# Sketched attention rebuilt around small TensorE tiles and VectorE transposes, with a 256-token first FFN group

## The chip, the cores and the metric

One core of one Trainium2 chip. The metric is the device time of one execution in microseconds (us). Times are medians over the executions of a kernel, each compared with executions of the kernel before on the same chip in the same rounds. Each run lists the span and clock of one core only, so there is no second die to compare it with, and a run counts as slow only when it lies over 1.5% above the fastest of its own kernel. The kernel before takes 137.7 us.

PE is the TensorE matmul stream, PEld its weight loads, DVE is VectorE, ACT is ScalarE, POOL is GpSimd, and SP is the engine that issues most transfers.

## The reference, cut to what matters

```python
# q, k, v: (4 batches, 4 heads, 1088 tokens, 32); S1, S2: (8, 32), float32
def phi(x):                                   # 8 x 8 = 64 features per token and head
    a = einsum('rd,bhsd->bhsr', S1, x)
    b = einsum('rd,bhsd->bhsr', S2, x)
    return einsum('bhsi,bhsj->bhsij', a, b).reshape(..., 64)
kv  = einsum('bhsf,bhsd->bhfd', phi(k), v)
z   = phi(k).sum(axis=2)
num = einsum('bhsf,bhfd->bhsd', phi(q), kv)
den = einsum('bhsf,bhf->bhs', phi(q), z) + 1e-6
x   = (num / den)                             # -> 4352 tokens x 128
h   = x @ w_in                                # 128 x 2048
out = (h - tanh(h)) @ w_out                   # 2048 x 128
```

All of `k` of a batch must be reduced into `kv` before any numerator of the batch exists, and `num/den` must exist before the feed-forward part (FFN) of those tokens can begin. With a group of 512 tokens, the FFN is 16 matmuls in, 16 tanh on ScalarE, 16 matmuls out, and two for the linear part `x @ w_in @ w_out`.

## The kernel before

The program is written as a list of operations with dependencies. A list scheduler in the kernel file, with a cost for each operation, fixes the order on each engine when the program is built. The list of an engine is its program, with semaphore waits between the operations. So an operation whose data is late holds up what stands behind it in the list.

The parts that the change touches, shortened:

```python
GCOLS = [512] * 8 + [256]          # token groups of the FFN
QG = [(0, 3), (3, 6), (6, 9)]      # pieces of 128-token blocks of one batch
...
bank_h = 3 PSUM banks; bank_o = 1; bank_kv = 1; bank_a = 3      # (names shortened)
...
# k: two sketches one after the other, all 128 rows, 32 columns
for x in range(2):
    pa = _Val(bank_a)
    for g in range(4):
        e.matmul(pa[g*32:(g+1)*32, 0:288], sab[:, x, :], t_[:, c0:c0+288])
    e.transpose(ab[:, x, :], pa[:, 0:288])                 # VectorE
...
# q: three sketches of the whole batch (a, b, and the one for the denominator)
# then for each piece of three blocks:
qp = ap * b                                                # VectorE outer product, 768 columns
for hp in range(2):
    for bi in range(nb):                                   # TensorE transposes with an identity
        e.transpose(tp[:, bi*128:bi*128+kk], qp[0:kk, ...], ident[0:kk, 0:kk])
    copy(qt[:, 0:ncol], tp[:, 0:ncol])                     # ScalarE or VectorE
for hp in range(2):                                        # numerator
    e.matmul(nm[hp*64:(hp+1)*64, 0:ncol], kvb[:, hp, :], qts[hp][:, 0:ncol])
copy(xT[:, col0:col0+ncol], nm[:, 0:ncol])
```

## Time and profile before

| what | measured | view |
|---|---|---|
| time | 137.7 us (137.01 to 138.67 over 5 runs) | times |
| span of the profiled run | 135.4 us | page, first line |
| first tanh | 31.26 us | timeline of ScalarE, chain |
| last output transpose | 131.38 us | timeline of VectorE |
| last numerator burst of batches 2 and 3 | 83.29 and 108.99 us, so 25.7 us a batch | timeline of TensorE |
| TensorE instructions, with weight loads | 982 + 996 = 1978 | page, section 1 |

The page of the kernel before divides the span into 40 slices of 3.4 us. Each digit is the busy share of a slice in tenths, and PEclk is the granted TensorE clock in tenths of full speed:

```profile
PE   0477977598989999999999999999999999989970
PEclk9999986869999999999999999999999999999999
DMA  4999999970406050005000220140003004013043
```

From slice 10 on, until the last two, TensorE is busy for 80% of a slice or more. Before that it often is not, and in slices 6 to 9 its clock is down to 0.8 and 0.6. The table of stretches of the kernel before gives the same with numbers (stretch, its length, then the busy time and count of PE, PEld, DVE, ACT and POOL, the granted clock, the DMA share and GB/s):

```profile
20.00:24.00 4.00, 2.75 (x24) 1.20 (x20) 2.38 (x11) 0.27 (x1) 0.00 (x0) 0.70 1.07 260
48.00:56.00 8.00, 7.95 (x43) 3.81 (x43) 6.04 (x16) 6.44 (x14) 0.00 (x0) 1.00 0.22 34
```

The chain of waits of the kernel before, in order of time, at the end of its start-up (start, duration, what):

```profile
27.48 2.32 PE psa L551 x8
29.80 1.44 PE psa L421 x16
31.26 0.61 ACT th L610
```

So the kernel before is a start-up of 31 us and a TensorE-bound stream of 100 us. The prediction rested on one more reading, the cost of changing between tile shapes on TensorE. This is a burst of 24 matmuls on 32-column tiles in the timeline of PE of the kernel before, amid FFN matmuls that start 0.22 us apart. The burst and its changes of shape take 63.78 − 63.08 = 0.70 us here. The profile puts 0.16 us of it down to a wait for ScalarE, and the prediction seems to leave that part out:

```profile
63.08 0.54 PE L443 MATMUL pskv<-w,v 128*32 128x64 f32 x24
63.78 0.38 PE L619 MATMUL pso<-th,wo 128*128 128x512 bf16 x1 [0.16 <-ACT th L610]
```

### The profile page before, as it was taken

To read this page: it belongs to the slowest core of one execution; us is meant where nothing else is said; L and a number is where in the kernel's file an instruction comes from. 1 tells how busy PE (TensorE), PEld (TensorE's weight loads), DVE (VectorE), ACT (ScalarE), POOL (GpSimd) and SP (SyncE) were. 2 spreads that over 40 slices of the span, in tenths; PEclk is the share of its full clock that TensorE was granted. 3 is DMA by queue.
4 is the path that set the end of the run, shared out by engine and by line. 5 is a ranking of instruction groups with operands and counts; after the bars stand their busy time and mean duration, and the time that the engine had idled before them with its cause. 6 is when DMAs were issued, how large, how long until landed. Compare 5 with 4: busy or idle time off the path is not lost.

```text
span 135.4 us, 2508 instructions
## 1 busy us (share of the span) xinstructions
PE 118.0 (87%) x982; PEld 54.8 (40%) x996; DVE 64.9 (48%) x152; ACT 89.4 (66%) x180; POOL 2.4 (2%) x22
## 2 busy tenths in 40 slices
PE   0477977598989999999999999999999999989970
PEld 0325623533344344434543535345334533333440
DVE  0447256958983698239056904561496131020210
ACT  3031670256964677976558797775579968999960
POOL 7000000000000000000000000000000000000000
PEclk9999986869999999999999999999999999999999
DMA  4999999970406050005000220140003004013043
GB/s 133 264 289 339 293 224 267 222 221 25 168 1 169 0 80 0 0 0 78 5 5 0 44 33 0 19 64 0 0 9 58 15 0 67 11 20 60 0 70 51
DMA packets 25563, 11.18 MB, mean 83 GB/s; under 512 B 18896, under 2 KB 22992, under 8 KB 25552
## 3 DMA queue, kind: packets, MB, share of 16 engines
q1 hardware_dynamic: 25472, 11.02, 34.9%
q8 instruction: 8, 0.13, 0.4%
q14 instruction: 3, 0.02, 0.1%
q10 hardware_dynamic: 80, 0.01, 0.0%
HBM read 8.79 MB, written 2.23 MB: 81 GB/s over the span
## 4 chain that ended last, share of the span: by engine, by line
PE 75%; ACT 11%; DVE 6%; DMA 2%; issue 2%; ACTq 0%
PE pso L619 19%; PE psh L607 19%; ACT th L610 11%; PE psa L551 7%; PE psa L541 7%; PE psa L500 5%; PE psa L421 5%; PE pskv L443 4%; PE pskv L453 3%; PE pso L623 3%; DMA s_86<-in_S_dram 2%; PE pskv L468 1%; PE psa L579 1%; DVE ot L628 1%; PE pskv L470 1%
## 5 line engine op out<-in xcount | busy, mean ns | idle before, releaser
L610 ACT ACTIVATE th<-psh 128x512 bf16<-128x512 f32 (+1 forms) x144 | 71.7, 592 | 19.0 <-PE psh L607 17.3
L607 PE MATMUL psh<-xT,wi 128*128 128x512 bf16 (+1 forms) x137 | 49.0, 368 | 1.2 <-ACT th L610 0.8
L619 PE MATMUL pso<-th,wo 128*128 128x512 bf16 (+1 forms) x138 | 45.5, 368 | 0.8 <-ACT th L610 0.7
L607 PEld LDWEIGHTS psh<-xT,wi 128*128 128x128 bf16 x144 | 13.9, 97 | 19.4 <-ACT th L610 9.6
L619 PEld LDWEIGHTS pso<-th,wo 128*128 128x128 bf16 x144 | 13.5, 99 | 19.1 <-issue 4.8
L628 DVE STREAM_TRANSPOSE ot<-pso 128x512 f32<-128x512 f32 (+1 forms) x9 | 6.1, 683 | 21.9 <-PE pso L619 21.9
L541 PE MATMUL psa<-ident,qp 128*128 128x128 f32 (+1 forms) x72 | 11.7, 289 | 2.5 <-DVE qp L530 2.3
L541 PEld LDWEIGHTS psa<-ident,qp 128*128 128x128 f32 (+1 forms) x72 | 9.0, 147 | 5.9 <-DVE qp L530 2.7
L530 DVE TENSOR_TENSOR qp<-ap,abq 128x768 f32<-128x768 f32 x12 | 11.1, 940 | 0.0
L432 DVE TENSOR_TENSOR w<-abk 128x768 f32<-128x768 f32 x12 | 10.8, 952 | 0.1
L277 DVE COPY qpT<-psa 128x320 f32<-128x320 f32 (+1 forms) x10 | 5.2, 518 | 11.8 <-PE psa L541 11.6
L551 PE MATMUL psa<-qpT,kvb 128*64 128x384 f32 (+1 forms) x48 | 10.0, 526 | 0.0
L504 DVE STREAM_TRANSPOSE abq<-psa 128x288 f32<-128x288 f32 x12 | 5.8, 483 | 7.5 <-PE psa L500 7.5
L443 PE MATMUL pskv<-w,v 128*32 128x64 f32 (+1 forms) x288 | 8.0, 247 | 1.3 <-DVE w L432 1.3
L277 ACT COPY qpT<-psa 128x384 f32<-128x384 f32 (+1 forms) x14 | 6.4, 481 | 3.9 <-PE psa L541 3.8
L443 PEld LDWEIGHTS pskv<-w,v 128*32 128x32 f32 (+1 forms) x288 | 5.4, 122 | 5.6 <-issue 2.9
L277 ACT CAST xT<-psa 128x384 bf16<-128x384 f32 (+1 forms) x10 | 4.6, 463 | 3.7 <-PE psa L551 3.3
L421 PE MATMUL psa<-kTa,sab 128*32 128x288 f32 x32 | 6.0, 483 | 1.1 <-DVE kTb L407 1.1
L570 ACT CAST wi<-wi_f 128x512 bf16<-128x512 f32 x4 | 2.5, 619 | 5.9 <-DMA wi_f<-in_moe_w_in_dram 5.7
L459 DVE TENSOR_TENSOR gm<-pskv,mask_84 32x32 f32<-32x32 f32 x4 | 0.7, 179 | 11.3 <-PE pskv L453 11.3
L421 PE MATMUL psa<-kTb,sab 128*32 128x288 f32 x32 | 6.0, 483 | 0.0
L425 DVE STREAM_TRANSPOSE abk<-psa 128x288 f32<-128x288 f32 x8 | 3.8, 480 | 4.0 <-PE psa L421 4.0
(63 smaller groups left out, 82.2 us busy)
## 6 DMA issues: line engine op xcount, KB each, us to landing
qL<-in_q_dram SPq DMA_DIRECT2D x8, 272.0 KB, 7.1
out_dram<-ot SPq DMA_DIRECT2D x20, 64.0 KB, 2.0
kLa<-in_k_dram SPq DMA_DIRECT2D x4, 288.0 KB, 6.0
v<-in_v_dram SPq DMA_DIRECT2D x8, 144.0 KB, 5.5
kLb<-in_k_dram SPq DMA_DIRECT2D x4, 256.0 KB, 5.3
v<-in_v_dram SPq DMA_DIRECT2D x8, 128.0 KB, 5.7
wi_f<-in_moe_w_in_dram SPq DMA_DIRECT2D x4, 256.0 KB, 5.4
wo_f<-in_moe_w_out_dram SPq DMA_DIRECT2D x4, 256.0 KB, 8.1
```

What stands on the lines that cost most here:

```text
L277: return e.copy(o, i) if name == "scalar" else e.tensor_copy(o, i)
L421: i = e.matmul(pa.ap[g * 32:(g + 1) * 32, 0:288], sab.ap[:, x, :], t_.ap[:, c0:c0 + 288], start=True, stop=True)
L432: P.add("vector", lambda e, n, p=p, wv=wv: e.tensor_tensor(out=wv.ap.rearrange("p (x i j) -> p x i j", i=8, j=8), in0=ab.ap[:, 0, p * 96:( ...
L443: i = e.matmul(kv.ap[h * 32:(h + 1) * 32, 0:64], vt.ap[0:kk, h, blk * 32:(blk + 1) * 32], wv.ap[0:kk, (bi * 4 + h) * 64:(bi * 4 + h + 1) * ...
L500: i = e.matmul(pa.ap[g * 32:(g + 1) * 32, 0:288], s_, qv[:, :, g, :], start=True, stop=True)
L530: P.add("vector", lambda e, n, sl=sl, aq=aq, qp=qp, nx=nx: e.tensor_tensor(out=qp.ap[:, 0:nx * 64].rearrange("p (x i j) -> p x i j", i=8, ...
L541: P.add("tensor", lambda e, n, bi=bi, kk=kk, tp=tp, hp=hp, qp=qp: e.transpose(tp.ap[:, bi * 128:bi * 128 + kk], qp.ap[0:kk, bi * 256 + hp ...
L551: i = e.matmul(nm.ap[hp * 64:(hp + 1) * 64, 0:ncol], kvb.ap[:, hp, :], qts[hp].ap[:, 0:ncol], start=True, stop=True)
L607: P.add("tensor", lambda e, n, jb=jb, hv=hv: e.matmul(hv.ap[:, 0:n_], wi[jb // 4].ap[:, (jb % 4) * 128:(jb % 4 + 1) * 128], xt, start=True ...
L610: P.add("scalar", lambda e, n, hv=hv, th=th: e.activation(out=th.ap[:, 0:n_], in_=hv.ap[:, 0:n_], func=AF.Tanh, scale=-1.0), r=[hv], w=[th ...
L619: fn = lambda e, n, x=x, st=st, sp_=sp_: e.matmul(ov.ap[:, 0:n_], wo[x // 4].ap[:, x % 4, :], ths[x].ap[:, 0:n_], start=st, stop=sp_)
L628: P.add("vector", lambda e, n: e.transpose(ot.ap[:, 0:n_], ov.ap[:, 0:n_]), r=[ov], w=[ot], key=t0, cost=_dve(n_))
```

## The change

The intent is to take attention work off TensorE and to let the FFN begin earlier.

- Both sketches of k (and of q) come from one burst on eight 64x32 tiles that run side by side.
- The denominator comes from a Gram matrix of the two k sketches, gathered over four column groups.
- The outer products of q are transposed in 32x32 blocks by VectorE instead of by TensorE. The numerator is a burst of 64 short matmuls on all sixteen 32x32 tiles.
- Sketches, kv, Gram and numerator share one fixed set of four PSUM banks, `bk[0..3]`. The numerator writes all four.
- The first FFN group has 256 tokens, and q of batch 0 is loaded, sketched and finished in three pieces.
- All loads are queued at the start, since k, v and q have a buffer for every batch. Zero matmuls fill long waits of TensorE.

The diff, cut to its core (the scheduler's new cost tables, `weights()`, the loads and most of the VectorE operations are left out):

```diff
-GCOLS = [512] * 8 + [256]
-QG = [(0, 3), (3, 6), (6, 9)]
+GCOLS = [256] + [512] * 7 + [384, 128]
...
+    psa = ps("psa", 4)
+    bk = [_Val(ap=psa[:, i * 512:(i + 1) * 512], psum=True) for i in range(4)]
...
+        def sk(e, n):                                     # both sketches of k
+            for g in range(4):
+                for rh in range(2):
+                    i = e.matmul(psa4[g * 32:(g + 1) * 32, rh, 0:288], wab.ap[rh * 64:(rh + 1) * 64, :],
+                                 kT.ap[rh * 64:(rh + 1) * 64, g * 288:(g + 1) * 288], start=True, stop=True)
+            return i
+        P.add(_pe(540), sk, r=[kT, wab], w=[bk[0], bk[1]], key=key - 1000, mode="64x32")
...
-                    P.add("tensor", lambda e, n, ...: e.transpose(
-                        tp.ap[:, bi * 128:bi * 128 + kk], qp.ap[0:kk, ...], ident.ap[0:kk, 0:kk]),
-                        r=[qp, ident], w=[tp], key=kg, cost=109)
-                P.add(both(ncol), ... copy(e, n, qt.ap[:, 0:ncol], tp.ap[:, 0:ncol]), r=[tp], w=[qt], key=kg)
+                    P.add(_v(cn * 256), lambda e, n, qp=qp, qt=qt, c0=c0, c1=c1, cn=cn: e.transpose(
+                        qt.ap[:, c0 * 256:c1 * 256], qp.ap[:, 0:cn * 256]), r=[qp], w=[qt], key=kg + 200)
...
-                for hp in range(2):
-                    i = e.matmul(nm.ap[hp * 64:(hp + 1) * 64, 0:ncol], kvb.ap[:, hp, :], qts[hp].ap[:, 0:ncol], ...)
+                    for x in range(2):
+                        for h in range(4):
+                            for g in range(4):
+                                i = e.matmul(psa4[h * 32:(h + 1) * 32, g, 0:nb * 32],
+                                             kvb.ap[g * 32:(g + 1) * 32, x, h * 32:(h + 1) * 32],
+                                             qq[g * 32:(g + 1) * 32, 0:nb, h, x, :], start=(x == 0), stop=(x == 1))
+                P.add(_pe(...), num, r=[kvb, qt], w=bk, key=kg + 300, mode="32x32")
...
-        q_side(b, sc, kvb)
+            q_side(b, sc, kvb, [(0, 2), (2, 5), (5, 9)], [(0, 2), (2, 5), (5, 9)], k0 + 5000)   # batch 0
+            q_side(b, sc, kvb, [(0, 9)], [(0, 5), (5, 9)], kd + 6000)                           # other batches
...
-    P.schedule()
+    P.schedule(filler)
```

## The prediction

> **What bounds it now.** After a start-up, TensorE. By stretches, PE is busy 7.5 to 8.0 us of every 8 from 48 to 128 us; ScalarE 4.8 to 7.9, VectorE 0.7 to 6.7. The chain of waits is 75% PE. In the timeline the first tanh (L610) starts at 31.26 us and the last output transpose at 131.4: 31 us of start, 100 us of PE-bound stream, 4 us of tail. Span 135.4, time about 2.3 more.
>
> The 100 us: 8.5 token groups x 34 matmuls at 0.216 us (the spacing of L607 and L619 in the timeline) = 62.4. The rest is attention, about 11.5 us of PE per batch in the chain: k sketches 1.24, kv 1.6, Gram 0.87, small ones 0.6, q sketches 1.66, transposes (L541) 2.0, numerator (L551) 3.6.
>
> **What changes on PE, per batch.** The 18 transposes go (VectorE takes them). Sketches: eight 64x32 tiles give both sketches in one burst, 16 short instructions instead of 16 of the full depth: 1.24 -> 0.6 for k, 1.1 -> 0.6 for q. Gram: rotates over four column groups, 0.87 -> 0.5. Numerator: 3.6 us -> two bursts of 32 matmuls on 32x32 tiles. The kv bursts (L443) run four column tiles side by side at 14 ns from start to start; I take 8 to 12 ns with sixteen tiles, 0.5 to 0.8 us a burst. Against this stands the change of tile mode. [...] round an L443 burst of 0.33 us of starts PE loses about 0.09 us before and 0.2 after, so the slot is 0.56 to 0.63. With nine bursts a batch I get 7.3 us instead of 11.5.
>
> **VectorE.** Gains the transposes of the outer products (2304 columns a batch, 2.6 us by L488's 1.3 ns a column), loses most PSUM copies; about 17.7 us a batch by the durations of the groups. It stays below PE (15.6 + 7.3 = 23 us) but not by much; a batch is also a serial chain of about 20 us. ScalarE loses the qpT copies: 68 us of tanh (0.49 each) plus 5 of copies.
>
> **Start.** Before, all of batch 0 runs before the first tanh, at a granted clock of 0.70 to 0.87 from 16 to 32 us (table of stretches). After, the first group is 256 tokens, its attention only two blocks; loads all go first, and zero matmuls fill PE's waits. [...] My chain: k landed 5.3, sketch 6.9, outer products 10.7, kv matrix ready 12.7, weight casts 13.7, sketch of q 14.3, numerator 17.4, first tanh about 18. That saves 13 us.
>
> **Sum.** Start 18; PE stream 63 (FFN, small groups a little dearer) + 3 x 7.3 + 3 for the rest of batch 0 = 88; stalls 3 to 4, chiefly where batch 1's numerator waits for VectorE near 35 to 40 us; tail 3. Span about 111, time 113 us. PE remains the limit; ScalarE alone would end near 92.
>
> **What would show it.** First tanh at 17 to 20 us. Numerator bursts at most 0.8 us of starts. Clock near 1.0 from 6 us. PE still over 90% busy after 25 us; VectorE busy about 75 us.
>
> **What would make it wrong.** (a) Tile bursts limited by issue (20 ns each makes the numerator 1.3 us, +4 us in all) [...]. (b) VectorE's serial chain longer than the FFN of a batch: PE waits, 118 to 122. (c) Bursts cheaper and start at 16: 105 to 107. (d) Loads later than assumed, since everything is queued at once.
>
> Predicted 113 us, 8 in 10 between 105 and 121; faster 0.98, within 2% 0.01, slower 0.01.

Three passages are cut, where marked: what a change of tile shape does inside TensorE (twice), and a rule of what idleness and activity do to the clock. The trace of the kernel before shows the delays around the bursts and a clock of 0.70 to 0.87 from 16 to 32 us. Start 18, stream 88, stalls 3 to 4 and tail 3 add up to 112 to 113 us; the author put the span at about 111 and the time at 113. The times behind the arrows, the 8 to 12 ns with sixteen tiles and the chain of the start are estimates. The first two seem to set out from the times before the arrows and from the 14 ns of L443. The 20 ns of (a) is a case assumed for the reckoning (the third L443 burst of a batch averages 20 ns in the trace of the kernel before).

## The result, and the profile after

The changed kernel takes 130.84 us (130.32 to 132.79 over 5 runs) against 137.7 us. The ratio is 0.949, with an interval of 0.942 to 0.956. It is faster by 5%, where 18% was predicted, and outside the predicted range of 105 to 121 us. Ratios here are always the mean time of one kernel's fast runs over that of the other's fast runs of the same rounds, so they are not quite the ratio of the medians that are quoted.

The profiled run of the changed kernel is one of the two of five that count as slow (span 130.5 us at a mean clock of 0.96, where the three others have 128.5 to 129.1). The times inside the changed kernel that are quoted below come from this slow run, so in sum they can be up to 2 us too long; where these 2 us lie was not traced. No conclusion below rests on that difference: the same stretches appear in the fast profiled runs of the experiments (e2, which keeps the order of all engines, has its long gap too, 5.31 us).

From its page, the slices and the transfers of instructions. The last two lines are the queue q8, which the page calls instruction, the first of the two from the page before, the second from the page after (packets, MB, share of 16 engines):

```profile
PE   6998989674048899899899999999999999999990
PEclk9999999999855699999999999999999999999999
DMA  2999999999700000040000410400040130401322
```

```profile
q8 instruction: 8, 0.13, 0.4%
```

```profile
q8 instruction: 12, 0.20, 0.7%
```

TensorE is now busy for 80% or more from slice 13 on, and partly or wholly idle in slices 8 to 12. The table of stretches after (columns as before):

```profile
28.00:32.00 4.00, 2.21 (x91) 1.25 (x91) 2.98 (x7) 0.48 (x1) 0.00 (x0) 1.00 1.07 239
32.00:36.00 4.00, 0.00 (x0) 0.00 (x0) 3.74 (x9) 0.00 (x0) 0.00 (x0) 0.84 0.80 173
36.00:40.00 4.00, 1.76 (x72) 1.28 (x81) 1.07 (x2) 0.73 (x3) 0.00 (x0) 0.50 0.06 16
40.00:44.00 4.00, 4.00 (x54) 1.06 (x38) 2.93 (x6) 2.15 (x4) 0.00 (x0) 0.50 0.00 0
```

From 32 to 36 us TensorE does nothing, and for the 8 us after that its clock is half. The timeline of PE after shows what happens to the three pieces of batch 0 (start, busy time, line, operation, then the idle time before it and what ended it):

```profile
20.01 0.85 PE L636 MATMUL psa<-qpT,kvb 32*32 32x64 f32 x64
21.34 0.40 PE L570 MATMUL psa<-qT,wab 64*32 64x96 f32 x16
...
28.62 0.96 PE L636 MATMUL psa<-qpT,kvb 32*32 32x96 f32 x64 [0.67 <-DVE qpT L628]
...
30.15 0.45 PE L570 MATMUL psa<-qT,wab 64*32 64x128 f32 x16
30.54 0.43 PE L582 MATMUL psa<-qT,sc 128*32 128x128 f32 x8
37.12 1.52 PE L636 MATMUL psa<-qpT,kvb 32*32 32x128 f32 x64 [6.16 <-DVE qpT L628]
```

The numerators (L636) of the three pieces come at 20.0, 28.6 and 37.1 us, 8.5 us apart. Between two of them stands the sketch of the next piece (L570), and after each sketch VectorE's whole chain for that piece (7.3 us from sketch to numerator for the second piece, 7.0 for the third). The first FFN group needs only the first piece. It has 256 tokens, about 4 us of TensorE (34 matmuls, 0.11 us apart in the timeline). The second group needs all three pieces, so the stream proper begins at about 39.8 us, with batch 1's k sketch. The prediction had it follow the first tanh at 18 us with stalls of 3 to 4 us.

What TensorE does once it streams came close to the prediction in sum. The lines below are the timeline of PE around one of the larger numerators, in the middle of batch 2:

```profile
75.20 0.38 PE L699 MATMUL psh<-xT,wi 128*128 128x512 bf16 x1
75.51 1.18 PE L636 MATMUL psa<-qpT,kvb 32*32 32x160 f32 x64
76.84 0.38 PE L699 MATMUL psh<-xT,wi 128*128 128x512 bf16 x1 [0.16 <-issue]
```

One matmul of this form takes 0.305 us, so 64 of them start 14 ns apart ((1.18 − 0.305)/63). The 128-column burst of 1.07 us, with 0.27 us for one matmul, gives about 13 ns, and batch 0's 64-column burst of 0.85 us, with 0.225, about 10. The prediction took 8 to 12. The first numerator of batches 2 and 3 starts at 75.51 and 98.02 us, so a batch now takes 22.5 us instead of 25.7.

Splitting each span by the first FFN matmul and the end of the last gives the sum that has to be explained:

| | start | FFN and the rest on TensorE | tail | span |
|---|---|---|---|---|
| predicted | 18 | 88 + 3 to 4 of stalls | 3 | about 111 |
| after, profiled run | 22.0 | 105.5 (21.97 to 127.52) | 3.0 | 130.5 |

The start is 4 us later than predicted, and between the first and last matmul of the FFN there are 14 us that the prediction did not have (12 to 13 if the fast runs' spans are shorter in this stretch).

### The profile page after: what moved, and what is told of

Its sections match the earlier page's. It is cut to its first block, busy times and chain, and to the rows that moved or that the text cites. A ratio compares the mean times of both kernels' runs of the same rounds, so it can differ in the third digit from the quotient of the medians.

```text
span 130.5 us, 3757 instructions
## 1 busy us (share of the span) xinstructions
PE 111.9 (86%) x1602; PEld 54.7 (42%) x1618; DVE 72.1 (55%) x155; ACT 85.2 (65%) x189; POOL 1.8 (1%) x14
## 4 chain that ended last, share of the span: by engine, by line
PE 48%; SPq 12%; DVE 12%; ACT 11%; DMA 11%; issue 3%
PE pso L712 16%; PE psh L699 16%; SPq L393 12%; DMA qL<-in_q_dram 11%; ACT th L702 10%; PE psa L636 6%; PE psa L532 3%; DVE w L522 3%; PE pso L716 2%; PE psa L491 2%; DVE abk L496 2%; DVE ot L721 1%; DVE qT L559 1%; PE psa L570 1%; ACT xT L318 1%
## 5 line engine op out<-in xcount | busy, mean ns | idle before, releaser
L702 ACT ACTIVATE th<-psh 128x512 bf16<-128x512 f32 (+3 forms) x160 | 72.0, 566 | 10.2 <-PE psh L699 9.3
L699 PE MATMUL psh<-xT,wi 128*128 128x512 bf16 (+3 forms) x152 | 51.9, 353 | 2.7 <-ACT th L702 1.2
L712 PE MATMUL pso<-th,wo 128*128 128x512 bf16 (+3 forms) x154 | 49.3, 349 | 1.1 <-issue 0.5
L721 DVE STREAM_TRANSPOSE ot<-pso 128x512 f32<-128x512 f32 (+3 forms) x10 | 6.3, 635 | 25.7 <-PE pso L712 25.7
L636 PE MATMUL psa<-qpT,kvb 32*32 32x128 f32 (+3 forms) x576 | 10.1, 294 | 6.8 <-DVE qpT L628 6.8
L367 PE MATMUL pso<-zz 128*128 128x256 bf16 x86 | 12.6, 296 | 1.1 <-DVE zz L366 1.1
L628 DVE STREAM_TRANSPOSE qpT<-qp 128x512 f32<-128x512 f32 (+1 forms) x16 | 11.5, 755 | 0.1
L623 DVE TENSOR_TENSOR qp<-ap,abq 128x512 f32<-128x512 f32 (+1 forms) x16 | 11.3, 744 | 0.2
L636 PEld LDWEIGHTS psa<-qpT,kvb 32*32 32x32 f32 x576 | 6.6, 106 | 10.4 <-DVE qpT L628 7.5
L367 PEld LDWEIGHTS pso<-zz 128*128 128x128 bf16 x86 | 8.6, 106 | 3.2 <-DVE zz L366 1.1
L532 PE MATMUL psa<-w,vL 128*32 128x64 f32 x288 | 6.5, 223 | 1.2 <-DVE w L522 1.2
```

The lines of the kernel that those rows point to most:

```text
L367: filler = (lambda e, n: e.matmul(bank_o.slots[0][0][:, 0:256], zz.ap[:, 0:128], zz.ap[:, 128:384], start=True, stop=True), zop, bank_o)
L532: i = e.matmul(psa4[h * 32:(h + 1) * 32, 2, 0:64], vL[b][:, h, blk * 32:(blk + 1) * 32], wv.ap[:, (bi * 4 + h) * 64:(bi * 4 + h + 1) * 64] ...
L623: P.add(_v(cn * 256), lambda e, n, aq=aq, qp=qp, av=av, c0=c0, c1=c1, cn=cn: e.tensor_tensor(out=qp.ap[:, 0:cn * 256].rearrange("p (x i j) ...
L628: P.add(_v(cn * 256), lambda e, n, qp=qp, qt=qt, c0=c0, c1=c1, cn=cn: e.transpose(qt.ap[:, c0 * 256:c1 * 256], qp.ap[:, 0:cn * 256]), r=[q ...
L636: i = e.matmul(psa4[h * 32:(h + 1) * 32, g, 0:nb * 32], kvb.ap[g * 32:(g + 1) * 32, x, h * 32:(h + 1) * 32], qq[g * 32:(g + 1) * 32, 0:nb, ...
L699: P.add(_pe(n_ / 2.4 + 2.6), lambda e, n, jb=jb, hv=hv: e.matmul(hv.ap[:, 0:n_], wi[jb // 4].ap[:, (jb % 4) * 128:(jb % 4 + 1) * 128], xt, ...
```

## The experiments

All are edits of the changed kernel. All 14 gave the reference's result within tolerance, except one. Medians of the kernel before were 137.55 (e1 to e4), 137.78 (e5 to e8), 138.13 (e9 to e12) and 138.28 us (e13, e14). The theories for the missing time, by the letters that the expectations use:

- A: VectorE's list holds the block transposes of batches 1 and 2 ahead of batch 0's last piece, and these wait for late loads.
- B: VectorE has too much work in that stretch, whatever its order.
- C: the half clock after TensorE's long idle time.
- D: the first sketch waits for all of batch 0's q, though it needs a third.
- E: the three pieces of batch 0 run one after the other, since they share the four PSUM banks.

A sixth, F, came out of the results of e5 to e8.

### e1_moved: VectorE's transposes for later batches taken out of the way

The chain of waits after had suggested A, as its longest piece at this point is a load of q for a later batch, which VectorE waits for before going on with batch 0:

```profile
18.13 14.00 DMA qL<-in_q_dram
32.13 0.02 issue
32.15 0.85 DVE qT L559
33.00 0.17 DVE m L598
```

```diff
+    late = [o for o in dv if o.name in ("pk1", "pq1", "pk2", "pq2")]   # k and q transposes of batches 1, 2
+    # ... placed right behind batch 0's last outer-product transpose in VectorE's list
```

> Edit: in VectorE's queue alone, the block transposes of k and q of batches 1 and 2 that stand among batch 0's work are put behind batch 0's last transposed outer product. Theory A (VectorE's queue is in order, and these transposes, with the late loads that they wait for, stand in front of batch 0's last numerator): about 8.5 us of such stretches leave batch 0's chain between 20 and 34 us, PE's 6.2 us gap shrinks below 2 us, the clock no longer halves; time 119 to 124 us (130.5 for the changed kernel's fast runs). Rival B (VectorE has too much work in that stretch, whatever the order): the transposes have to be done all the same before batch 1, time 128 or more.

Measured: 129.67 us (129.53 to 129.99), ratio 0.942. The last numerator of batch 0 came at 34.45 us instead of 37.12, and TensorE's wait before it shrank from 6.16 to 4.33 us, but the clock still fell to half, and the time fell by about 1 us, for which the intervals of the two ratios (0.934 to 0.949, and 0.942 to 0.956) overlap. A is real in the order of events and small in time, and theory A as the main cause fell.

### e2_nowait: the same list, but nothing to wait for

```diff
-  e.transpose(kT.ap[:, lo:hi], kL[b][:, lo:hi])
+  e.transpose(kT.ap[:, lo:hi], kL[0][:, lo:hi])     # batch 0's data, which is there (q likewise)
```

The result is wrong (relative error 1.13). Order and amount of work are those of the changed kernel.

> Edit: order of all engines unchanged; the block transposes of batches 1 to 3 read batch 0's loaded k and q, which have landed long before (result wrong on purpose). It takes away the wait for late loads and leaves the work and the order. Theory A with the loads as the cause: VectorE's 3 us of waits between 20 and 33 us go and the halved clock with the shorter gap: 125 to 128 us. If it is only the order of work: 129.5 to 130.5.

Measured: 131.36 us (130.76 to 132.5), ratio 0.954, no gain, and above both forecast ranges. The last numerator of batch 0 came at 35.5 us, 1.6 us earlier than in the changed kernel's profile; but that profile is of a slow run with a span 0.9 us longer, so how much of it is real is open. Late loads in VectorE's list are not what the time is lost to.

### e3_warm: TensorE kept busy in the gap

```diff
+    # 50 zero matmuls (128x256) in TensorE's list just before batch 0's last numerator
```

> Edit: 50 matmuls of zeros (128x256) put into PE's queue where it sits idle before batch 0's last numerator; nothing else changes. Theory C (the gap of 6.2 us also halves PE's clock from 36 to 45 us, and this is on the critical path): 126.5 to 128.5 us, clock 1.0 in 36 to 44 us. Rival: VectorE and ScalarE bound this stretch, the halved clock costs nothing: 130 to 131.

Measured: 129.11 us (128.64 to 130.41), ratio 0.938. The mean clock rose to 0.993, and the last numerator took 1.07 us instead of 1.52. So the cold clock (C) costs about 1.7 us, at the edge of the noise (the ratios' intervals, 0.931 to 0.946 and 0.942 to 0.956, overlap), and is a consequence of the gap, not its cause. The time lies between the two forecasts.

### e4_splitq: the first sketch waits for its own piece of q

```diff
+            for a, z, t_ in qtr:                 # transposes of q's load pieces
+                if z <= s0 * 4 or a >= s1 * 4:   # columns that this sketch does not read
+                    o_.deps.pop(t_, None)
```

> Edit: the sketch of q's first two blocks of batch 0 no longer waits for the transposes of all three pieces of q, only for its own (the scheduler then orders anew). Theory D (the start is late, first tanh 22.3 us, because the first sketch waits for q's third piece, landed at 15.1): first tanh 17 to 19 us; the time falls by 3 to 4 us if the start is on the critical path, to 126.5 to 127.5. Rival A alone: batch 0's last numerator still waits for VectorE's later transposes whose loads land when they did: the time stays within 1 us of 130.5 although the first tanh is earlier.

Measured: 127.21 us (126.91 to 127.58), ratio 0.923. The first tanh came at 19.89 us instead of 22.29, and the numerators at 17.61, 24.52 and 32.50 us. The time matches what was expected; the first tanh is 0.9 us later than that. D is worth 3.6 us, because the whole series of pieces begins earlier, but the pieces are still 7 to 8 us apart.

### e5_onesketch: batch 0's q sketched in one burst

```diff
-            q_side(b, sc, kvb, [(0, 2), (2, 5), (5, 9)], [(0, 2), (2, 5), (5, 9)], k0 + 5000)
+            q_side(b, sc, kvb, [(0, 9)], [(0, 2), (2, 5), (5, 9)], k0 + 5000)
```

With one sketch, no later sketch has to wait until a numerator has left the shared banks, and VectorE can run the three pieces back to back. The scheduler also orders anew here: the transposes for batch 1 that stood between the pieces move behind the third one or ahead of the first numerator. e1 and e6 hold this fixed.

> Edit: batch 0's q is sketched in one burst of nine blocks, as in the other batches, not in three bursts; the three numerators and the small first group stay. Theory E (the three pieces of batch 0 run one after the other, because each next sketch needs the PSUM banks that the numerator before it holds until its copy is done; so batch 0's last numerator comes at 37 us, and only then can the 512-token groups start): the last numerator of batch 0 at 26 to 29 us, time 119 to 123. Rival A (late loads in front of it in VectorE's queue): last numerator at 32 or later, time 126 or more.

Measured: 126.94 us (126.39 to 127.46), ratio 0.920. The mechanism of E was right: the numerators came at 23.15, 25.82 and 28.24 us, 2.5 us apart instead of 8.5. But the time did not follow. A new gap stood in TensorE's timeline, waiting for nothing that the profile shows:

```profile
23.15 0.85 PE L636 MATMUL psa<-qpT,kvb 32*32 32x64 f32 x64 [0.85 <-DVE qpT L628]
...
25.82 0.96 PE L636 MATMUL psa<-qpT,kvb 32*32 32x96 f32 x64
...
28.24 1.07 PE L636 MATMUL psa<-qpT,kvb 32*32 32x128 f32 x64
29.24 0.28 PE L699 MATMUL psh<-xT,wi 128*128 128x256 bf16 x1
32.95 0.37 PE L699 MATMUL psh<-xT,wi 128*128 128x256 bf16 x1 [3.43 <-issue]
```

The clock was 0.50 from 32 to 36 us and 0.66 from 36 to 40.

### e6_onesketch_moved: e5 and e1 together

> Edit: the one sketch of e5, and also e1's edit (block transposes of batches 1 and 2 behind batch 0's last transposed outer product). Theory E alone: within 1.5 us of e5, the gain of e1 again. If late loads hold the queue after all: 3 us or more under e5.

Measured: 125.97 us (125.16 to 127.33), ratio 0.912. The numerators came at 22.2, 24.9 and 27.3 us, yet the next burst, the k sketch of batch 1, still stood at 33.74 us (its profiled run is the one of its four that counts as slow, by 1.7% over the fastest). Work that is ready a microsecond earlier is not started earlier, so VectorE is not the one that holds TensorE there. Against e1, which has the same transposes moved and three sketches (numerators at 19.88, 27.78 and 34.45 us), the single sketch alone brings the pieces from 7 to 8 us apart to 2.5.

### e7_two_sketches: two sketches, the first on its own piece of q

```diff
-            q_side(b, sc, kvb, [(0, 2), (2, 5), (5, 9)], [(0, 2), (2, 5), (5, 9)], k0 + 5000)
+            q_side(b, sc, kvb, [(0, 2), (2, 9)], [(0, 2), (2, 5), (5, 9)], k0 + 5000)
```

It also has e4's edit, and a DMA rate in the scheduler's cost table lowered from 285 to 240.

> Edit: batch 0 sketched as two blocks and then seven, the first not waiting for the rest of q (e4's edit), and the scheduler told a DMA rate of 240 in place of 285 bytes per ns, so that it counts on the loads when they land. Theory E with D: first tanh 17 to 19 us and last numerator of batch 0 at 25 to 28: 117 to 121 us. If the early first group is worth nothing, as theory E has it for the stream, it is equal to e5 within 1.5 us.

Measured: 125.44 us (124.41 to 125.77), ratio 0.908. The first tanh came at 19.5 us, and again TensorE stopped with "issue" as the reason, for 1.24 us until 32.24. The last numerator of batch 0 began at 29.8 us, not at 25 to 28, and the time missed its range of 117 to 121 us; it is within 1.5 us of e5, as forecast for an early first group that is worth nothing. This time the stop lay in the middle of a numerator burst, between two of its 64 matmuls. The 64 are one operation of the list, and the program places its semaphore waits before the first of them, so there is none to wait for between them. That is what led to theory F: TensorE has run out of instructions.

The count supports this. The table of stretches from 0 to a given time counts matmuls and weight loads. In e5, e6, e7 and e10 the last stop comes after 955 of them, whatever the instruction is. In the changed kernel and in e1 there is a shorter stop of 1.04 and 1.06 us that ends near 24.7 us, after 699. (The profile puts that one down to a tanh, but all tanh issued by then had ended 0.66 us before it was over.) The difference is 256. (Waits and other sequencer instructions are not in these counts.)

### e8_512_first: no small first group

```diff
-GCOLS = [256] + [512] * 7 + [384, 128]
+GCOLS = [512] * 8 + [256]
-    qp_p = pool("qp", 3, [128, 3 * 256])
+    qp_p = pool("qp", 4, [128, 3 * 256])          # needed for this order to be free of races
-            q_side(b, sc, kvb, [(0, 2), (2, 5), (5, 9)], [(0, 2), (2, 5), (5, 9)], k0 + 5000)
+            q_side(b, sc, kvb, [(0, 9)], [(0, 5), (5, 9)], k0 + 5000)
```

> Edit: groups as before the change (eight of 512 tokens, one of 256), batch 0 in one sketch and two numerators like the other batches (and a fourth outer-product buffer, which the check asks for). Theory E: the small first group buys little; first tanh near 25 us, stream whole from 29: 119 to 123 us, that is, faster than the changed kernel by 7 or more although its first tanh is 3 us later. Rival (an early first tanh is what the change lives from): 131 or more.

Measured: 123.05 us (122.74 to 124.14), ratio 0.894. The first tanh came only at 28.27 us, 6 us later than in the changed kernel, and still the time was nearly 8 us shorter. There was no gap and the clock was 0.999. So an early first tanh is not what the time depends on; what the small group is worth alone is seen in e11. This kernel passes instruction 955 only at 35.98 us.

### e9_gated and e10_control: loads held back, or not

Both have e5's single sketch, and each later batch's k and q transposes are placed behind the previous batch's last outer-product transpose in VectorE's list. They differ in one thing. In e9 the last 14 loads (of batches 2 and 3) are not queued at the start but released one at a time, one after every third tanh from the seventh on:

```diff
+    ths_ = [o for o in P.order["scalar"] if o.name == "th"]
+    lds_ = [o for o in P.order["sync"] if o.name == "load"][-14:]
+    for i, o in enumerate(lds_):
+        o.deps[ths_[6 + 3 * i]] = True            # e9 only
```

The refill that theory F speaks of is the 16 KB packet of queue q8, looked up below. That it queues behind the loads was a theory.

> Base: e5 (one sketch for batch 0), with every batch's k and q block transposes put behind the last transposed outer product of the batch before. Edit: the 14 loads of batches 2 and 3 are held back and released one by one by every third tanh from the seventh on, so that the DMA queues are short while PE runs batch 0. Theory F (in e5 PE sits 3.4 us before 32.95 us with no semaphore to wait for, because the 16 KB refill of its instructions queues behind megabytes of loads; the clock then halves): the gap shrinks to under 0.5 us, no half clock; against e10 (same order, no holding back) 4 to 6 us less, about 120 us. Rival (the gap is something else, or the loads slow what they feed): equal to e10 or slower.

> Control for e9: e5 with the same order of VectorE's transposes, loads all at the head of the queue as in the changed kernel. Theory F: the gap of about 3 us before 33 us stays, 125 to 126.5 us.

Measured: e9 120.89 us (119.92 to 121.04), ratio 0.8745 with an interval of 0.8704 to 0.8787. e10 126.59 us (126.54 to 126.8), ratio 0.918. Holding the loads is worth 5.7 us. About 1.1 us of it lies before the gap, where the first tanh comes at 23.26 instead of 24.34 us; the rest comes at the gap and after it. e10's timeline of PE:

```profile
27.79 1.07 PE L636 MATMUL psa<-qpT,kvb 32*32 32x128 f32 x64
28.79 0.28 PE L699 MATMUL psh<-xT,wi 128*128 128x256 bf16 x1
32.49 0.37 PE L699 MATMUL psh<-xT,wi 128*128 128x256 bf16 x1 [3.41 <-issue]
```

The table of stretches of e10, from 0 to two times on either side of the gap, shows that PE (477) and PEld (477, 478) issued one instruction between them, 955 in all:

```profile
0.00:28.80 28.80, 26.66 (x477) 18.22 (x477) 20.34 (x48) 10.85 (x23) 1.81 (x14) 1.00 0.98 267
0.00:32.40 32.40, 26.94 (x477) 18.32 (x478) 21.29 (x50) 11.73 (x26) 1.81 (x14) 0.98 0.99 262
```

And e9's timeline of PE at the same place in the program, where it goes on through instruction 955 (passed at 27.99 us) without a wait:

```profile
26.72 1.07 PE L636 MATMUL psa<-qpT,kvb 32*32 32x128 f32 x64
27.72 0.53 PE L699 MATMUL psh<-xT,wi 128*128 128x256 bf16 x2
28.08 0.27 PE L712 MATMUL pso<-th,wo 128*128 128x256 bf16 x1
28.19 0.28 PE L699 MATMUL psh<-xT,wi 128*128 128x256 bf16 x1
```

The DMA view shows when a packet of the instruction queue q8 is moved. Each is 16 KB (16384 bytes in the traces before and after). In e10 one falls in the window from 29.5 to 30.0 us, among loads at more than the full share of the engines (first fence, from the window 28 to 33 us). In e9 it falls in the window from 25.0 to 25.5, and loads take 8% from 25 to 28 us (second fence):

```profile
q1 hardware_dynamic: 809, 1.22, 103.9%
q8 instruction: 1, 0.02, 1.6%
```

```profile
q1 hardware_dynamic: 11, 0.05, 8.1%
q8 instruction: 1, 0.02, 2.3%
```

Put beside the time at which TensorE passes instruction 699, this holds in every trace in which it was looked up (times from the table of stretches, packets to half a microsecond from the DMA view):

| kernel | loads of batches 2, 3 | passes 699 | next q8 packet starts | delay | passes 955 | stop there |
|---|---|---|---|---|---|---|
| e9 | held | 24.35 | 25.0 to 25.5 | about 1 | 27.99 | none |
| e11 | held | 25.96 | 26.5 to 27.0 | about 1 | 34.06 | none |
| e14 | held | 25.81 | 26.5 to 27.0 | about 1 | 29.84 | none seen |
| e10 | all queued | 25.44 | 29.5 to 30.0 | 4.1 to 4.6 | 32.49 | 3.41 |
| e5 | all queued | 25.88 | 30.0 to 30.5 | 4.1 to 4.6 | 32.96 | 3.43 |
| e7 | all queued | 25.13 | 29.5 to 30.0 | 4.4 to 4.9 | 32.26 | 1.24 |
| e8 | all queued | 27.44 | 31.0 to 31.5 | 3.5 to 4 | 35.98 | none |
| after | all queued | 24.71 | 29.0 to 29.5 | 4.3 to 4.8 | 37.21 | hidden by the wait for VectorE |

So with all loads queued, the next q8 packet started 3.5 to 5 us after TensorE had passed 699; with the loads held back, about 1 us. In e10, e5 and e7, which came to 955 at about 29 to 31 us, TensorE stopped there; in e8, which passed it only at 35.98 us, it did not. One more thing ties the stops to the packets. Read from the packets' own start and duration in the traces, TensorE goes on 1.35 to 1.70 us after the packet has landed in all six of these stops (after 955 in e5, e6, e7 and e10, after 699 in the changed kernel and e1), though the stops last from 1.04 to 4.22 us. In none of the 15 kernels does it pass 699 or 955 sooner than 1.3 us after the landing; e9, which does not stop, passes 955 after 1.47. That these packets bring the instructions TensorE waits for, and stand in line behind the loads, is the reading that fits these lines. The traces show the delay and the effect of holding the loads, not the line itself.

### e11_512_gated: the held loads without the small first group

e8 with e9's VectorE order and held loads.

> Base: e8 (groups of 512 first, batch 0 in one sketch and two numerators), with e9's order and e9's holding back of the loads of batches 2 and 3. e8 shows no such gap, so theory F gives it little: 121.5 to 123 us; if VectorE gains by the order of its transposes, or the first numerator comes earlier with fewer loads in the queues, 119 to 121.

Measured: 121.33 us (121.13 to 121.4), ratio 0.879, clock 0.998. It is about as fast as e9, so with the gap gone, the small first group makes no difference of note. Holding the loads, with the new order of VectorE, gains less here (1.7 us from e8), as expected of a kernel that did not stop.

### e12_no_filler: without the zero matmuls

```diff
-    P.schedule(filler)
+    P.schedule(None)
```

> Edit: the changed kernel without the zero matmuls that fill PE's waits at the start. It says what the filler is worth. If a halved clock at the start costs what the kernel before showed (0.70 to 0.87 granted from 16 to 32 us): first tanh 1 to 2 us later and 131.5 to 133 us. If batch 0 is bound by VectorE and loads anyway: 130 to 131.

Measured: 132.39 us (131.88 to 133.07), ratio 0.961, so the filler is worth about 1.6 us. This part of the change does what it was meant to do in the first 30 us (the clock of the changed kernel was 1.00 in every stretch of 4 us from 0 to 32 us, where the kernel before had 0.70 to 0.87 from 16 to 32), but it does not reach into the gap after 31 us.

### e13_gated_three: held loads with the three serial pieces

The changed kernel with e10's VectorE order and e9's held loads.

> Edit: the changed kernel with batch 0 still in three sketches and three numerators, VectorE's transposes in e10's order, the loads of batches 2 and 3 held back as in e9. If E and F are in series (the refill's gap lies hidden in the wait for the third numerator, save 1 us at 23.7): 127 to 129.5 us, last numerator of batch 0 at 32 to 34. If F was the whole cause and E only came with it: 121 to 123 us.

Measured: 128.66 us (127.97 to 129.06), ratio 0.934. The last numerator still came at 34.02 us, after 4.33 us of waiting for VectorE. This completes a square:

| | loads all queued | loads held |
|---|---|---|
| three sketches | 130.8 (after) | 128.7 (e13) |
| one sketch | 126.6 (e10) | 120.9 (e9) |

The changed kernel alone has the old order of VectorE, which is worth about 1 us (e1). With e1 (129.7) in its place, holding the loads alone gives 1.0 us, one sketch alone 3.1, both 8.8. The two losses lie over each other. In the changed kernel TensorE waits for VectorE's third piece until 37.12 us, and the q8 packet that started at 29.5 us had landed by 30.9 us, within that wait; once the pieces come early, TensorE stops in the open after 955 (3.41 us in e10). In e13 TensorE's own list adds to the series: VectorE had the second piece ready at 26.15 us, but its numerator stands behind the FFN of the first group and came at 27.36.

### e14_two_gated: an earlier first tanh on top

e7 with e9's VectorE order and held loads.

> Edit: e7 (two blocks sketched first without waiting for the rest of q, then seven) with e10's order of transposes and the loads held back as in e9. If the late first sketch costs time by itself: first tanh near 19 us, last numerator of batch 0 near 26, time 117 to 119.5. If batch 0's last numerator sets the time and it comes no earlier than in e9 (26.7 us): 120 to 121.5.

Measured: 122.03 us (121.55 to 122.2), ratio 0.885, no better than e9 and rather slower, and above both forecast ranges. The first FFN matmul came at 19.5 us instead of 22.9, but the last numerator of batch 0 at 29.2 us instead of 26.7. The span divides as follows:

| | start | to the end of the last FFN matmul | tail | span |
|---|---|---|---|---|
| e9 | 22.9 | 92.2 (22.94 to 115.13) | 3.0 | 118.1 |
| e14 | 19.5 | 97.9 (19.52 to 117.42) | 3.0 | 120.4 |

The earlier start is paid back in full in the stretch after it. And even with the loads of batches 2 and 3 held, TensorE stopped once in this kernel with no releaser, for 0.96 us inside its first numerator, after 444 matmuls and weight loads, 255 before 699:

```profile
16.93 0.31 PE L644 MATMUL psa<-qpT,kvb 32*32 32x64 f32 x6
18.20 0.80 PE L644 MATMUL psa<-qpT,kvb 32*32 32x64 f32 x58 [0.96 <-issue]
```

The loads of the first batches are still in the queue at that time (mean DMA share 0.91 from 0 to 17.03 us and 0.93 from 0 to 18.75). So e14 is not quite the clean test of an earlier start that it was meant to be.

## Why the prediction was right or wrong

**Direction and the steady state: right.** The period of a batch is 22.5 us (15.6 + 7.3 = 22.9 predicted, 25.7 before). The prediction gave TensorE 88 us of work, "FFN, small groups a little dearer) + 3 x 7.3 + 3". In e9, which has no long stop, the stretch from the first to the last FFN matmul is 92.2 us, where 88 and 3 to 4 of stalls were predicted. The changed kernel itself does not show this: from 39.8 us to the last FFN matmul it needs 87.8 us (127.52 − 39.76), but that stretch has neither the first group nor batch 0's attention. By the prediction's own terms it should be about 81 (an estimate: 63 less half of one of 8.5 groups, and 3 x 7.3). That it comes near 88 is chance.

**Numerator bursts: right to a tenth.** "At most 0.8 us of starts" was predicted. Measured were 0.80 us for 128 columns (1.07 less one matmul's 0.27) and 0.87 for 160.

**Change of tile shape: seen, and in the stream dearer than assumed.** The slot of a 160-column burst is 76.84 − 75.51 = 1.33 us for 0.87 us of starts, so the next matmul starts about 0.45 us after the burst's last; before the burst there are about 0.09 us more than usual (75.51 − 75.20, less the usual 0.22). In all six bursts between FFN matmuls the delay after is 0.43 to 0.45 us. After batch 0's first two bursts it is only 0.15 and 0.17 us (20.80 and 29.52 us), though a 128x128 tile follows there too, so the change of shape alone does not explain it. The prediction had 0.2 after and 0.09 before. It seems to have taken 0.16 us after the burst in the kernel before as a wait for ScalarE; the same 0.16 us stands here after the burst with no releaser, so that wait was perhaps not the cause there. The period of a batch came out right all the same; which term made up for it was not looked up.

**VectorE: right in sum, wrong in one place.** It is busy for 72.1 us (75 predicted) and does not bound the stream. But point (b) of what might go wrong, VectorE's serial chain, came true for batch 0 alone.

**The step that failed: "Start 18" and "stalls 3 to 4, chiefly where batch 1's numerator waits for VectorE near 35 to 40 us".** The prediction followed the chain to the first tanh and let TensorE's stream run from there. But the first group is a token group of 256, about 4 us of work, and all groups behind it need batch 0's other two pieces. Those were never costed as a chain of their own. They measured 8.5 us each. In the program a sketch writes banks that the numerator before it fills and a copy must first empty, so it cannot run ahead (TensorE's weight loads for the second and third sketch waited 0.6 us in all for ScalarE's copy xT), and VectorE's chain of 7 us begins anew behind it. Instead of 3 to 4 us of stalls there were 17 (105.5 − 88, in the slow profiled run; 15 to 16 if the fast runs' spans are shorter in this stretch). e5 showed the serial pieces by removing them: 8.5 us apart became 2.5. The wait was also not batch 1's numerator but batch 0's own.

**"First tanh at 17 to 20 us": wrong.** It came at 22.29, 4 us after the 18 of the predicted chain, as the first sketch waited for all of q. e4 brought it to 19.89. The diff shows the cause: one value `qT` for three load pieces.

**"Clock near 1.0 from 6 us": wrong.** It was 0.50 from 36 to 44 us. In this trace TensorE sat idle for 6.16 us, until 37.12 us, and the clock fell to half within that time (0.84 in the mean from 32 to 36 us, 0.50 from 36 to 44). The stream began at 39.8 us, and the clock was full only from 45 us on, after about 5 us (0.53 from 44 to 45 us, 1.00 from 45 to 46). With zero matmuls in the gap, the mean clock of the run was 0.993 (e3). The half clock cost about 1.7 us (e3), at the edge of the noise. The prediction reckoned with a lowered clock only for the start.

**What was missing altogether: by theory F, the instructions themselves.** The change raises TensorE's instructions from 1978 to 3220 (1602 + 1618), and the 16 KB instruction packets from 8 to 12, while it also queues all loads at once. TensorE stopped after 955 matmuls and weight loads for 1.24 to 3.43 us (e5, e7, e10; 4.22 in e6, in a run that counts as slow), and for 1.04 us after 699, 256 earlier, in the changed kernel. With all loads queued the next q8 packet started 3.5 to 5 us after 699 was passed, with them held about 1 us. Risk (d), "loads later than assumed", named the queueing of everything at once, but the wrong victim. In the changed kernel as it stands this loss is mostly covered by the serial pieces; it shows in full only when those are cured.

**The rest.** The fastest version here, e9, is 120.89 us and correct, against a prediction of 113. Its stream and tail are as predicted, and its 5 us (22.9 against 18) lie in the start. In e14 an earlier first group alone did not win them back, as batch 0's last numerator then came later; how much of that the stop of 0.96 us in e14 cost is open. Whether a faster chain for all three pieces would was not tried.

## What to carry to other kernels

When a change lets the first small piece of work start earlier, follow the chain to the second and third piece too: what counted here is when the stream could run without a break, and the pieces that shared PSUM banks ran in series, 8.5 us apart. A change that multiplies small instructions (here 1978 to 3220 on TensorE) should be checked for stops with no releaser at fixed distances of the instruction count (here after 699 and 955), above all while many loads are queued; releasing late loads one by one behind the compute cost nothing here and won 5.7 us where TensorE had stopped in the open (1 to 2 us elsewhere). When a cure of one clear wait gains less than that wait, look for a second loss hidden under the first before giving up the theory.
